# An attention and feed-forward kernel: 15 products for 18 in the feed-forward, key sums on column strips, an inverse root through logarithms

## The chip, the cores and the metric

The kernel runs on one core of one Trainium2 chip. The metric is the time of one execution on the device, in microseconds (us), as the median of several. One execution of each kernel is also recorded by the hardware profiler; its length is called the span and is 1.5 to 3 us under the timed run. The engines are TensorE (PE; PEld are its weight loads), VectorE (DVE), ScalarE (ACT), GpSimd (POOL) and SyncE (SP), which here only issues transfers. A name with a q at its end, such as ACTq, is an engine's own instruction queue issuing transfers.

## The reference, cut

```python
# q, k, v: (8, 12, 448, 64) float32; the weights are float64: 768x1536 twice, 1536x768
rms = np.sqrt(np.mean(x * x, axis=-1, keepdims=True) + 1e-06)
q_n, k_n = q / rms_q * g_q, k / rms_k * g_k          # condensed
attn = np.exp(scale * q_n @ k_n.T - max); attn /= attn.sum(-1) + 1e-9   # condensed
x = (attn @ v) as (B*S, H*D) = 3584 x 768            # condensed
g = x @ w_gate
silu = g * (1.0 / (1.0 + np.exp(-g)))
val = x @ w_val
return (silu * val @ w_out).astype(np.float32)
```

## The kernel before

The program is four blocks of two batches. A block has the gate and value ("up") products, then the output ("down") products. Among the down products of blocks 0, 1 and 2 lies the attention of the next two batches, 12 pairs of heads each: these are the mixed stages. The attention of the first two batches comes ahead of everything, the "early part". Weights are float64 and are converted once, early and beside block 0. A planner in the program lists every operation with a planned cost and time and emits them in an order that it works out; `order.add("DVE", 0.64, when, emit, after=[...])` is one such entry.

The inverse root of the norms, a power on GpSimd:

```python
def inverse():
    rr = take("rr", m, [P, 2 * NC])
    nc.gpsimd.tensor_tensor(out=rr, in0=tiles["ss", m][:, 0], in1=minus_half, op=ALU.pow)
...
rr = add("POOL", 5.2, ready - 14.0, inverse, after=[sums], ...)
```

The sums over keys, four products on 64x64 quarters of TensorE, whose two halves are added and inverted over all 448 queries:

```python
for x in range(2):
    for h in range(2):
        nc.tensor.matmul(
            to[ds(D * h, D), x, 0:S], ones[ds(D * x, D)],
            tiles["sums", m][ds(D * x, D), h], start=True, stop=True,
        )
...
def copy_den():
    nc.scalar.copy(take("inv", m, [P, S]), tiles[den][:, 0, 0:S])

def invert():
    inv = tiles["inv", m]
    nc.vector.tensor_tensor(out=inv, in0=inv, in1=tiles[den][:, 1, 0:S], op=ALU.add)
    nc.vector.reciprocal(inv, inv)
```

The up products, 7 for each 2x2x2 split, with three differences of weights per half-block made on GpSimd:

```python
for to, a, b in ((T1, B12, B11), (T2, B22, T1), (T4, B21, T2), (B12, B22, B12)):
    load = add("POOL", 0.93, ..., lambda ...: nc.gpsimd.tensor_tensor(..., op=ALU.subtract), ...)
...
for c in range(NK):
    nc.tensor.matmul(
        into[:, 0:S], w[:, side, c, :], xs[:, side, c],
        start=(fresh and c == 0), stop=(c == NK - 1), ...
    )
```

## Time and profile before

Three runs: 1548.67 to 1549.82 us, median 1549.4.

| stage | us in the trace |
|---|---|
| early part, to the first dense up product | 138.5 |
| block 0, to the up products of block 1 | 377.9 |
| block 1 | 369.2 |
| block 2 | 370.7 |
| block 3 and the end | 291.6 |
| span | 1547.9 |

A stage begins where the first up product of its block begins. The prediction shows the busy shares, the chain and the stage windows. One view that it doesn't show, the groups of instructions, has the two that the argument needs; the columns are line, engine, operation, out<-in, count | busy us, mean ns of one | idle us of the engine before them and what ended most of it:

```profile
L940 POOL TENSOR_TENSOR rr<-ss,minus_half 128x28 f32<-128x28 f32 x36 | 179.8, 4996 | 122.8 <-DVE ss L934 122.8
L1010 ACT ACTIVATE es<-st 128x896 f32<-128x896 f32 x108 | 95.2, 914 | 137.7 <-PE at L1068 63.2
```

A power over 28 columns costs GpSimd 5.0 us. ScalarE idled 137.7 us before the exponentials, its largest work, and TensorE waited for them only 6.0 us in the whole run: in the mixed stage that the prediction shows, ScalarE is free for more than half of the time.

### The profile page before, as it was taken

Reading aid. Unit: us, or ns where it says so; the run is one execution under the profiler, and the core shown is the slowest. Engines: PE = TensorE matmul, PEld = TensorE weight load, DVE = VectorE, ACT = ScalarE, POOL = GpSimd, SP = SyncE. Lnnn points to the kernel's source line nnn. Section 1 sums busy time; section 2 is a strip of 40 time slices with the busy share of each in tenths; the row PEclk is TensorE's granted clock in tenths of the full one; section 3 lists DMA queues with packets and bytes.
Section 4 is the critical chain, followed back from the end, with each engine's and each line's share of the span. In section 5 each row is a group of like instructions: output and inputs, shape, how many; then the busy total and the mean of one; then the engine's idle time right before and its main releaser. Section 6 shows DMA issues by size and latency. Waiting matters only on the chain.

```text
span 1547.9 us, 17349 instructions
## 1 busy us (share of the span) xinstructions
PE 1507.7 (97%) x6384; PEld 742.4 (48%) x6384; DVE 892.6 (58%) x1053; ACT 449.6 (29%) x761; POOL 726.4 (47%) x440
## 2 busy tenths in 40 slices
PE   6998999999999999999999999999999999999998
PEld 2333544444454555544444555544444455555555
DVE  5999767876676434446777633345577753433221
ACT  6865324334442101233443101013534310000000
POOL 5881356676775222565775332355668433232000
PEclk9999999999999999999999999999999999999999
DMA  6655778734432212333543211233353311111232
GB/s 175 191 169 186 247 232 254 228 111 111 123 79 90 61 41 73 78 78 73 125 94 101 72 43 52 62 80 74 81 120 87 121 61 41 56 47 42 97 112 79
DMA packets 250307, 164.43 MB, mean 106 GB/s; under 512 B 187749, under 2 KB 240229, under 8 KB 249445
## 3 DMA queue, kind: packets, MB, share of 16 engines
q1 hardware_dynamic: 241600, 152.21, 35.1%
q10 hardware_dynamic: 8612, 11.02, 2.1%
q8 instruction: 52, 0.85, 0.2%
q14 instruction: 43, 0.34, 0.1%
HBM read 133.30 MB, written 29.88 MB: 105 GB/s over the span
## 4 chain that ended last, share of the span: by engine, by line
PE 73%; DVE 2%; ACT 1%; DMA 0%; issue 0%; SPq 0%; ACTq 0%; DVEq 0%
PE mm L1318 37%; PE mm L1499 24%; PE st L999 5%; PE at L1068 5%; PE st L1081 2%; ACT es L1010 1%; DVE hs L1467 0%; DMA ws<-out_sides 0%; DVE inv L1114 0%; DVE gt L1467 0%; DVE xs L1155 0%; SPq L886 0%; DVE sums L1021 0%; DVE rows L1576 0%; DVE xs L1123 0%
## 5 line engine op out<-in xcount | busy, mean ns | idle before, releaser
L1318 PE MATMUL mm<-xs,ws 128*128 128x448 f32 x2016 | 764.3, 541 | 8.4 <-DVE xs L1155 4.9
L1318 PEld LDWEIGHTS mm<-xs,ws 128*128 128x128 f32 x2016 | 382.5, 190 | 388.9 <-issue 370.3
L1302 POOL TENSOR_TENSOR ws<-ws 128x384 f32<-128x384 f32 x192 | 207.1, 1089 | 397.5 <-DMA ws<-quarters 350.7
L1499 PE MATMUL mm<-ws,gt 128*128 128x384 f32 x912 | 302.6, 489 | 0.0
L940 POOL TENSOR_TENSOR rr<-ss,minus_half 128x28 f32<-128x28 f32 x36 | 179.8, 4996 | 122.8 <-DVE ss L934 122.8
L1499 PEld LDWEIGHTS mm<-ws,gt 128*128 128x128 f32 x912 | 171.0, 190 | 132.9 <-issue 12.0
L1010 ACT ACTIVATE es<-st 128x896 f32<-128x896 f32 x108 | 95.2, 914 | 137.7 <-PE at L1068 63.2
L1015 POOL TENSOR_TENSOR sums<-es 128x896 f32<-128x896 f32 x36 | 78.2, 2173 | 103.4 <-PE st L1081 50.1
L999 PE MATMUL st<-QT,KT 64*64 64x448 f32 (+1 forms) x1152 | 114.0, 501 | 6.2 <-ACT es L1010 6.0
L1336 DVE TENSOR_TENSOR s<-s,mm 128x448 f32<-128x448 f32 x96 | 59.5, 620 | 99.7 <-PE mm L1318 99.6
L1114 DVE RECIPROCAL inv<-inv 128x448 f32<-128x448 f32 x36 | 106.3, 2953 | 1.2
L1336 DVE TENSOR_TENSOR wide<-s,mm 128x448 f32<-128x448 f32 x72 | 44.7, 621 | 97.7 <-PE mm L1318 97.5
L1336 DVE TENSOR_TENSOR gt<-s,mm 128x448 f32<-128x448 f32 x72 | 44.6, 620 | 93.9 <-PE mm L1318 93.8
L1499 PE MATMUL mm<-ws,hs 128*128 128x384 f32 x288 | 96.4, 490 | 0.0
L1359 ACT COPY s<-mm 128x448 f32<-128x448 f32 x48 | 25.5, 532 | 238.7 <-PE mm L1318 238.7
L1068 PE MATMUL at<-es,v 64*64 64x448 f32 x864 | 88.8, 537 | 0.9 <-DVE xs L1120 0.9
L955 POOL TENSOR_TENSOR t<-qk,rr 128x448 f32<-128x448 f32 x72 | 78.0, 1104 | 1.3
L1015 POOL TENSOR_TENSOR sums<-sums,es 128x896 f32<-128x896 f32 x36 | 75.1, 2086 | 2.8
L1423 ACT ACTIVATE wide<-gt 128x1344 f32<-128x1344 f32 x24 | 31.7, 1323 | 152.8 <-DVE gt L1336 152.7
L1499 PEld LDWEIGHTS mm<-ws,hs 128*128 128x128 f32 x288 | 53.9, 190 | 42.2 <-DVE xs L1120 3.5
L1576 DVE TENSOR_TENSOR rows<-part,mm 128x384 f32<-128x384 f32 x56 | 30.6, 547 | 66.9 <-PE mm L1499 51.2
L1120 DVE TENSOR_TENSOR xs<-xs,at 128x448 f32<-128x448 f32 x36 | 22.3, 619 | 78.0 <-ACT xs L1117 78.0
(93 smaller groups left out, 1352.4 us busy)
## 6 DMA issues: line engine op xcount, KB each, us to landing
ws<-quarters SPq DMA_DIRECT2D x48, 768.0 KB, 4.4
ws<-out_sides SPq DMA_DIRECT2D x28, 1152.0 KB, 6.3
out_sides<-hs SPq DMA_DIRECT2D x6, 1536.0 KB, 6.0
qk<-in_q_dram SPq DMA_DIRECT2D x144, 56.0 KB, 3.0
qk<-in_k_dram SPq DMA_DIRECT2D x144, 56.0 KB, 2.5
out_dram<-rows ACTq DMA_DIRECT2D x42, 192.0 KB, 1.9
stage<-in_moe_w_val_dram SPq DMA_DIRECT2D x10, 768.0 KB, 6.5
v<-in_v_dram SPq DMA_DIRECT2D x72, 96.0 KB, 2.3
```

The costliest lines, as they stand in the source:

```text
L940: nc.gpsimd.tensor_tensor(out=rr, in0=tiles["ss", m][:, 0], in1=minus_half, op=ALU.pow)
L955: nc.gpsimd.tensor_tensor(out=tiles["t", m][:, x], in0=tiles["qk", (m, x)], in1=rr.to_broadcast([P, NC, C]), op=ALU.mult,)
L999: nc.tensor.matmul(st[ds(D * x, D), h, 0:n], tiles["KT", m][rows, ds(P * j + D * of_keys, D)], tiles["QT", m][rows, ds(Q * of_queries, n)] ...
L1010: nc.scalar.activation(e, tiles["st", (m, j)][:, :, 0 : S * width(j) // P], AF.Exp)
L1015: nc.gpsimd.tensor_tensor(out=to, in0=tiles["e", (m, 0)] if j == 1 else to, in1=e, op=ALU.add)
L1068: nc.tensor.matmul(tiles["at", (m, x)][ds(D * h, D), queries], tiles["v", m][rows, j, h], tiles["e", (m, j)][rows, h], start=j == 0, stop= ...
L1114: nc.vector.reciprocal(inv, inv)
L1302: lambda to=to, a=a, b=b: nc.gpsimd.tensor_tensor(out=tiles[key][:, to], in0=tiles[key][:, a], in1=tiles[key][:, b], op=ALU.subtract,),
L1318: nc.tensor.matmul(into[:, 0:S], w[:, side, c, :], xs[:, side, c], start=(fresh and c == 0), stop=(c == NK - 1), skip_group_check=not fina ...
L1336: nc.vector.tensor_tensor(out=to(), in0=one(), in1=two[:, 0:S], op=ALU.add)
L1423: lambda: nc.scalar.activation(take(*wide, [P, 3 * S]), rest, AF.Tanh, scale=0.5),
L1499: nc.tensor.matmul(banks[bank][:, 0:HALF], of(g), w[:, ts(g, HALF)], start=(g == 0), stop=(g == NG - 1),)
```

## The change

It has four intents. The feed-forward is split 2x3x3 with 15 products in place of 18, where before it was 2x2x2 with 7 for 8. All attention, the early part too, runs on 64x64 quarters, and the sums over keys on strips of 128 rows by 32 columns; each gives its sum on 32 partitions, so only 224 columns need inverting, and ScalarE copies the inverse to the partitions that need it. The inverse root moves from GpSimd to ScalarE, as exp(-ln(x)/2), with a refinement on VectorE. In block 0, the rounding of the weights goes through PSUM, which is meant to keep VectorE from locking GpSimd out there. The diff has 1804 lines; its core, shortened:

```diff
-            nc.gpsimd.tensor_tensor(
-                out=rr, in0=tiles["ss", m][:, 0], in1=minus_half, op=ALU.pow
-            )
+        def estimate():
+            ss = of()
+            rr = take("rr", m, list(ss.shape))
+            nc.scalar.activation(rr, ss, AF.Ln, scale=GAIN**-2)
+            nc.scalar.activation(rr, rr, AF.Exp, scale=-0.5)
+        def improve(): ...                # three small VectorE operations
+        first = order.add("ACT", 0.5, when, estimate, ..., mode="logarithms")
 ... key sums of the pairs in the mixed stages
-                        to[ds(D * h, D), x, 0:S], ones[ds(D * x, D)],
-                        tiles["sums", m][ds(D * x, D), h], start=True, stop=True,
+                            to[ds(D * h + C * x, C)], ... many[:, 0:C],
+                            ... term[:, h, ts(x, Q)], start=..., stop=...,
+        def invert():
+            nc.vector.reciprocal(take("rd", m, [P, Q]), tiles[den])
+        def spread():
+            inv = take("inv", m, [P, S])
+            for h in range(2):
+                for x in range(2):
+                    for to in range(2):
+                        nc.scalar.copy(
+                            inv[ds(D * h + C * to, C), ts(x, Q)], tiles["rd", m][ds(D * h + C * x, C)]
+                        )
 ... up products: 15 steps x gate and value x 2 chunks, weight sides made once and stored
+                for c in range(NC2):
+                    nc.tensor.matmul(
+                        ps(), w[:, step % 5, which, c], xs[:, SLOT[x], c],
+                        start=fresh and c == 0, stop=c == NC2 - 1, skip_group_check=True,
+                    )
 ... rounding of the weights
+            if by_bank: ... to = tiles[bank] ...      # a PSUM bank
```

## The prediction

> **What bounds the kernel now.** I read the page's busy shares first, then the chain that ended last in order of time, then the busy time of each engine stage by stage, then the groups by form.
>
> ```profile
> PE 1507.7 (97%) x6384; PEld 742.4 (48%) x6384; DVE 892.6 (58%) x1053; ACT 449.6 (29%) x761; POOL 726.4 (47%) x440
> PE   6998999999999999999999999999999999999998
> ...
> PE 73%; DVE 2%; ACT 1%; DMA 0%; issue 0%; SPq 0%; ACTq 0%; DVEq 0%
> ```
>
> TensorE is busy 97% of 1547.9 us, and the chain that ended last runs over it. Its busy time is modelled, so I look at the pace too. In the chain in order of time:
>
> ```profile
> 516.54 157.99 PE mm L1318 x420
> ...
> 736.11 7.94 PE mm L1499 x24
> ...
> 1256.46 189.56 PE mm L1318 x504
> 1446.02 96.77 PE mm L1499 x300
> ```
>
> L1318 is the gate/value ("up") product, L1499 the output ("down") product. 157.99/420 = 0.376 us for each 448-column instruction, 96.77/300 = 0.323 us for each 384-column one: 0.84 ns a column, without gaps. So the kernel runs at TensorE's rate, and what counts is how many columns TensorE streams. The program is four blocks of two batches: up, then down with the attention of the next two batches mixed in. Up of blocks 1, 2, 3 starts at 516.5, 885.7 and 1254.9, a period of 369.2 us; before it come 12 pairs of heads of early attention and block 0; at the end, up 189.56 + down 96.77 + 5.1 us of last eviction and store.
>
> The other engines in an up stage and in a mixed stage (columns: stretch, length, then busy us of each engine):
>
> ```profile
> 516.50:690.00 173.50, 173.50 (x475) 87.46 (x475) 71.74 (x104) 26.30 (x50) 69.72 (x56) 1.00 0.26 66
> 712.00:885.00 173.00, 171.47 (x1115) 83.91 (x1108) 126.10 (x142) 64.99 (x121) 105.62 (x50) 1.00 0.38 94
> ```
>
> In the mixed stage VectorE is at 126.1/173 = 73%, ScalarE 38%, GpSimd 61%; in up 41%, 15%, 40%. None bounds. The early attention is different: pairs come every 10.6 us (the weighted sums of successive pairs start at 102.49, 113.10 and 123.59), TensorE has about 8.7 us of work in each, and from 40 to 60 us VectorE is busy 19.79 of 20 us. There several engines bind together, and up starts densely at 143.0 with two products (12 instructions) done, as if dense from 138.5.
>
> **What the Trainium skill says.** "FP8 and Floating Point Precision", TensorE Precision Notes: true FP32 takes four passes. The trace agrees: each product is two instructions of 0.376 us for 448 columns, 4 cycles a column at 2.4 GHz within 1%. "TensorEngine Tiling (Array Packing)", Available Configurations and Key Properties: 64x64 gives four tiles, 128x32 four column tiles, and a change of mode drains the array. The trace shows the first: 8 instructions of 448 columns on quarters take two rounds, 0.75 us; it has no 128x32. A cluster from 736.04+7.94 to 750.32 takes 6.34 us against 5.26+0.75 = 6.01 of streaming, so its changes cost about 0.33 us. "ScalarE: Activation LUTs", Table sets: exp and ln share a set, so the new Ln and Exp cost no reload between them; a load is 1283 ns, which the trace's one load shows too. "SBUF — State Buffer", Who interferes with whom: VectorE with two SBUF inputs and GpSimd exclude each other. The trace agrees: the same 448-element operation averages 877 ns with two SBUF operands (L1123), 619 ns with one in PSUM (L1120). Rounding through PSUM avoids that lock in block 0.
>
> **The change part by part.**
>
> Up: now 12 half-blocks x 7 products x 3 chunks x 2 = 504 instructions a block; then 4 groups x 15 products x gate and value x 2 chunks x 2 = 480. At 0.376 that is 180.5 against 189.6: 9.1 us less, four times, all on the path.
>
> Down: now 25 x 6 x 2 = 300 instructions of 384 columns, 96.8 us dense; then 15 x 2 halves x 4 x 2 = 240 of 448, 90.3 us: 6.5 us less, four times. The saving is partly that 3584 tokens are no longer cut into tiles of 128 with one unpaired.
>
> Attention on quarters, 36 pairs: scores and weighted sums stay 5.26 us. The key sums go from 0.75 us to one round of 224 columns twice, 8 instructions on four strips, 2 x 0.188 = 0.376 us. A cluster becomes about 6.01 - 0.376 + 0.33 + 0.2 for one more change of mode = 6.16, against 6.34: 0.2 us x 12 = 2 us a stage.
>
> Mixed stage: now 25 products at 7.94 per two = 99.2, + 12 x 6.34 = 76.1, = 175.3; measured 369.2 - 189.6 = 179.6, so 4.3 us of stalls and small gaps. Then 90.3 + 12 x 0.2 + 12 x 6.16 + 4.3 = 171. Block period 180.5 + 171 = 351.5, against 369.2: 17.7 us less, for two full blocks 35.4.
>
> Last block: 9.1 + 6.5, less about 1.2 for the added 32x32 transpose and 128-byte stores after the last product: 14.4 us less.
>
> Early 12 pairs: TensorE has 5.26 + 1.5 (four key blocks summed by strips) + 0.75 (spreading the reciprocals by product) + about 0.8 for mode changes = 8.3 us, and the two-way halves and 1.2 us of transposes go. VectorE loses half the reciprocal (2.95 to about 1.5, 224 elements) and the sums (1.15), gains two transposes (1.26), three small operations (0.6), a join (0.62): about 6.0 + 6 conversions x 3.7 us/12 = 7.9 against about 9. ScalarE: 7.0 + 1.2 of conversion. GpSimd loses the pow (3 to 5 us) and gains conversion sums. Three engines near 8.3 give about 9.7 us a pair, not the 10.6 of now; 14 + 12 x 9.7 = 130.5, + 8 us for the last pair's reciprocal, division and first side sum, because all first products now need both batches, where the old order began with the even batch: 139. Nothing won, nothing lost.
>
> Block 0: 18 of the 24 weight conversions fall here, each about 4 us of VectorE, 2.4 ScalarE and 7 GpSimd; with evictions (26 of 0.62 us in each of four groups, 65 us) VectorE has some 150 of 190 us. Four accumulators instead of two give each eviction more slack. I allow 12 us of stalls, where the old block 0 lost about 8. Start of up 1: 139 + 180.5 + 12 + 171 = 502.5 against 516.5: 14 us less.
>
> Sum: 1547.9 - 14 - 35.4 - 14.4 = 1484; the timed run is 1.5 above the span: 1485.6. I put 1487.
>
> Removed work that saves nothing by itself: 179.8 + 45.5 us of pow and 207 us of weight differences on GpSimd, and half of 106 us of reciprocals on VectorE; they lay beside TensorE. More DMA (weight sides 1280 KB for each 15 us, 85 GB/s; 128-byte stores) lies under what the page shows it can do, 254 GB/s.
>
> **The rivals.**
> 1. VectorE becomes the bound of the mixed stage. Worked from 126.1: -12 x (1.43 + 0.62) for reciprocal and its add, + 7 for the refinement, + 10 side sums x 0.62, + 7 for 32 evictions and transposes instead of 24, + 12 for the larger combinations of 1792 elements = about 134 of 171, 78%. That is up from 73% but still under TensorE; as queues are in order, some evictions will come late. If each of the 12 clusters lost 1 us: +36 over three stages, 1523.
> 2. ScalarE's new spreading copies (8 of about 0.33 us a pair), store issues (4 of 0.34 us where one was) and table switches delay the exps, and TensorE waits for score banks. Work: 65 + 31 + 2 + 16 = about 114 of 171, from 38% to 67%. For it: nearly all of the PE waits in mixed stages now are already on exps, 6.0 us in total. Against: ample room. Effect 5 to 15 us.
> 3. Block 0 and the early part become bound by conversion and start-up. The program's own planned times allow 10 us a pair instead of 8 and 20 us more for block 0. If early pairs took 11 us and block 0 stalled 25: +29, 1516.
> 4. Strips do not overlap as quarters do: 1.5 us instead of 0.376 in 36 clusters and 6 instead of 1.5 in 12 early ones: about +95, no gain at all. The skill speaks against it.
> 5. Everything overlaps better, since GpSimd's lock on VectorE nearly goes: stalls of 2 instead of 4.3 and an early pace of 9: 1468.
>
> **Range and chances.** The arithmetic on TensorE (36 + 26 us fewer in products) is nearly certain; stalls are not. 1466 to 1514 holds rivals 2, 5 and most of 3. Two per cent faster is 1518.4: only rivals 1 with 3, or 4, cross it. Faster 0.87, same 0.11, slower 0.02.
>
> **What would show it.** Up in the last block about 180.5 us with 480 instructions, the last down about 90.3 with 240; a period of about 351 between up stages; TensorE still about 97% busy and the chain on it; key sums of 8 instructions in about 0.4 us; VectorE under 80% in mixed stages. It is wrong if the period exceeds 358 with waits on VectorE or ScalarE, if the first dense up product starts well after 145, or if the strips take over 1 us.

## The result

The changed kernel takes 1591.17 us (median of 4, 1588.08 to 1595.54), the kernel before 1549.61 in the same rounds: ratio 1.0271, 95% interval 1.0246 to 1.0297, slower. The prediction, 1487 with a range up to 1514, is wrong.

The page of the changed kernel, busy us, share and count by engine, then two lines of the 40 equal slices in tenths:

```profile
PE 1464.4 (92%) x6672; PEld 686.0 (43%) x6672; DVE 903.3 (57%) x1405; ACT 784.7 (49%) x1452; POOL 404.3 (25%) x440
...
PE   3878889999888989999989989999999989999998
...
PEclk9788999999999999999999999999999999999999
```

TensorE has less work, as predicted, but is busy 92% and no longer 97%. GpSimd has 322 us less. ScalarE has 335 us more, 784.7 against 449.6. The slices that lost are in the early part and in the three mixed stages. The granted clock also dips in the early part.

Where do ScalarE's 335 us come from? Its groups, each of one form:

```profile
L978 ACT COPY spare<-rd 32x224 f32<-32x224 f32 x288 | 108.1, 375 | 53.8 <-DVE rd L963 48.1 <-DMA out_dram<-spare 1.3
L667 ACT ACT_TABLE_LOAD x48 | 61.6, 1283 | 0.9
L666 ACT ACT_TABLE_LOAD x47 | 60.3, 1283 | 3.9 <-DMA work<-in_k_dram 3.1
...
L1351 ACT ACT_TABLE_LOAD x9 | 11.5, 1283 | 6.2 <-DVE st L1135 6.1
```

The spreading copies (L978) were expected. The loads of function tables at L666 (the Ln) and L667 (the Exp after it) were not: 95 of them, 121.9 us, where the kernel before has one load in all. L1351 is the Silu. One pair of heads in the timeline (start us, length us, what):

```profile
428.74 0.92 ACT L843 ACTIVATE es<-st 128x896 f32<-128x896 f32 x1
429.67 1.28 ACT L666 ACT_TABLE_LOAD   x1
430.97 0.23 ACT L666 ACTIVATE rr<-ss 128x28 f32<-128x28 f32 x1
431.21 1.28 ACT L667 ACT_TABLE_LOAD   x1
432.50 0.23 ACT L667 ACTIVATE rr<-rr 128x28 f32<-128x28 f32 x1
432.64 0.53 ACT L843 ACTIVATE more<-st 128x448 f32<-128x448 f32 x1
```

An exponential of scores (L843) runs with a table that has Exp. The Ln loads another, the Exp after it loads again, and the next exponential of scores needs none. So the table in use for Exp didn't have Ln, and the one loaded for Ln didn't have Exp. Between the two exponentials of scores, which feed TensorE, lie 2.98 us (429.66 to 432.64), of which 2.57 are loads.

Who waits? TensorE's waits from 700 to 1260 us, which hold two mixed stages, the second of the changed kernel but for its last 51 us (what waited <- for what: us in total, times, longest us). In the kernel before:

```profile
PE st L999 <- ACT es L1010: 4.1, 12, 1.0
```

In the changed kernel:

```profile
PE st L828 <- ACT es L843: 18.9, 19, 3.9
```

The scores (st) wait for a bank that an exponential must first empty. This is the wait that the prediction's second rival named, 15 us more over this window. The mixed stage of block 1 (stretch, length, busy us of PE, PEld, DVE, ACT and POOL, clock, DMA share, GB/s) shows ScalarE at 121.94 of 173 us, 70%, with TensorE at 94%:

```profile
770.00:943.00 173.00, 162.34 (x1044) 71.82 (x1036) 113.98 (x166) 121.94 (x242) 66.35 (x38) 0.99 0.42 94
```

Two steps of the prediction already hold. The down products of the last block, in the chain in order of time, run at the rate assumed, 0.376 us an instruction:

```profile
1496.28 72.17 PE mm L1456 x192
```

An undisturbed cluster of attention is even shorter than predicted. One in the kernel before, with its key sums (L1081) and the next down product (L1499):

```profile
743.98 1.74 PE L999 MATMUL st<-QT,KT 64*64 64x448 f32 x16
...
749.41 0.98 PE L1081 MATMUL st<-sums,ones 64*64 64x448 f32 x8
750.32 0.91 PE L1499 MATMUL mm<-ws,gt 128*128 128x384 f32 x2
```

And one in the changed kernel, with its key sums on strips (L928):

```profile
783.93 1.74 PE L828 MATMUL st<-work 64*64 64x448 f32 x16
...
789.37 0.59 PE L928 MATMUL st<-sums,many 128*32 128x224 f32 x8
789.88 0.64 PE L1456 MATMUL mm<-hs,ws 128*128 128x448 f32 x1
```

From its first scores to the next down product the cluster takes 6.34 us before (750.32 - 743.98) and 5.95 us after (789.88 - 783.93).

### The profile page after: what moved, and what is told of

It is laid out like the page before. It is cut to its first block, busy times and chain, and to the rows that moved or that the text cites. A ratio compares the mean times of both kernels' runs of the same rounds, so it can differ in the third digit from the quotient of the medians.

```text
span 1593.7 us, 19444 instructions
## 1 busy us (share of the span) xinstructions
PE 1464.4 (92%) x6672; PEld 686.0 (43%) x6672; DVE 903.3 (57%) x1405; ACT 784.7 (49%) x1452; POOL 404.3 (25%) x440
## 5 line engine op out<-in xcount | busy, mean ns | idle before, releaser
L1277 PE MATMUL mm<-xs,ws 128*128 128x448 f32 x960 | 408.8, 548 | 21.8 <-DVE xs L1024 8.9
L1277 PE MATMUL at<-xs,ws 128*128 128x448 f32 x960 | 408.5, 549 | 3.8 <-DVE v L1244 3.2
L1277 PEld LDWEIGHTS mm<-xs,ws 128*128 128x128 f32 x960 | 183.9, 193 | 208.6 <-issue 170.0
L1277 PEld LDWEIGHTS at<-xs,ws 128*128 128x128 f32 x960 | 185.2, 193 | 188.7 <-issue 177.5
L783 POOL TENSOR_TENSOR work<-work,rr 128x448 f32<-128x448 f32 x96 | 101.5, 1076 | 649.9 <-DMA v<-in_v_dram 322.0
L828 PE MATMUL st<-work 64*64 64x448 f32 (+1 forms) x1536 | 165.4, 533 | 67.4 <-ACT es L843 31.6
L1456 PE MATMUL mm<-gt,ws 128*128 128x448 f32 x448 | 176.1, 544 | 0.8 <-DVE spare L1244 0.8
L1456 PE MATMUL mm<-hs,ws 128*128 128x448 f32 x384 | 154.3, 553 | 0.0
L1351 ACT ACTIVATE st<-gt 128x448 f32<-128x448 f32 x96 | 52.4, 547 | 196.2 <-DVE gt L1244 94.7
L843 ACT ACTIVATE es<-st 128x896 f32<-128x896 f32 x129 | 114.3, 913 | 50.8 <-PE at L904 20.8
L978 ACT COPY spare<-rd 32x224 f32<-32x224 f32 x288 | 108.1, 375 | 53.8 <-DVE rd L963 48.1
L1456 PEld LDWEIGHTS mm<-gt,ws 128*128 128x128 f32 x448 | 83.5, 190 | 84.6 <-issue 81.8
L1238 ACT COPY gt<-mm 128x448 f32<-128x448 f32 x80 | 42.6, 533 | 156.2 <-PE mm L1277 152.9
```

The source lines that it names most:

```text
L783: nc.gpsimd.tensor_tensor(out=tiles["t", m][:, x], in0=tiles["qk", (m, x)], in1=rr.to_broadcast([P, NC, C]), op=ALU.mult,)
L828: nc.tensor.matmul(st[ds(D * x, D), h, 0:n], tiles["KT", m][rows, ds(P * j + D * of_keys, D)], tiles["QT", m][rows, ds(Q * of_queries, n)] ...
L843: nc.scalar.activation(e, tiles["st", (m, j)][:, :, 0 : S * width(j) // P], AF.Exp)
L978: nc.scalar.copy(inv[ds(D * h + C * to, C), ts(x, Q)], tiles["rd", m][ds(D * h + C * x, C)])
L1238: nc.scalar.copy(to, ps)
L1277: nc.tensor.matmul(ps(), w[:, step % 5, which, c], xs[:, SLOT[x], c], start=fresh and c == 0, stop=c == NC2 - 1, skip_group_check=True,)
```

## The experiments

The theories, as the expectations call them: T1, the table loads are the loss; T2, ScalarE is overloaded by the new copies and stores, loads or not; T3, the early part is slower by its structure; T4, the planner was told 0.5 us for Ln and Exp and so chose a bad order. The first four runs below were made on one chip, with the kernel before at 1549.3 us beside them; the next four (e5 to e8) had it at 1549.98, e9 to e11 at 1549.57 and e12 at 1550.31, so medians can be set side by side to within about 1 us. In e1, e3, e6 and e8 the planner's list and costs stay as they are, so the order of the work does too; the other runs change entries, costs or times in the list, and with them the order. What an order alone can do, e10_plan shows: about 14 us.

**Run e1_one_set: one set of tables that has both functions.** The set is asked for by name before the first Ln or Exp and again after each Silu. Nothing else changes.

```diff
+    def both_functions():
+        if table[0] != "both":
+            nc.scalar.preload_act_table_set("natural_log_exp_and_others")
+            table[0] = "both"
+            both_functions()                       # before the Ln, and before each Exp of scores
             nc.scalar.activation(rr, ss, AF.Ln, scale=GAIN**-2)
+                table[0] = "silu"                  # after each Silu
```

> The changed kernel with one line more before each Ln and Exp that follows a Silu: the table set that holds both is loaded there, so the 96 loads for Ln and Exp fall to about 9, and nothing else changes. Theory T1 (the loads are the cause: 105 loads x 1.283 us = 135 us of ScalarE, in front of exps that TensorE waits for): about 1500 us, early pairs under 11 us apart instead of 12.7, period of a block 352 to 358 instead of 367, granted clock back to 0.99. T2 (ScalarE is overloaded by the 288 spreading copies, 108 us, and the store issues, the loads only fill gaps): 1570 or more, period 363 or more. T3 (the early attention on quarters and the later first product cost the time, not the loads): the first dense up product still starts after 165 and the time stays above 1560.

Measured: 1529.61 us (1527.89 to 1530.3), ratio to the kernel before 0.9873 (0.9857 to 0.989), that is 61.6 us less than the changed kernel and 19.7 less than the kernel before. The loads fall to 18 (9 of this set, 9 for Silu). ScalarE between two exponentials of scores:

```profile
411.29 0.23 ACT L674 ACTIVATE rr<-ss 128x28 f32<-128x28 f32 x1 [3.75 <-DVE ss L778]
411.55 0.23 ACT L675 ACTIVATE rr<-rr 128x28 f32<-128x28 f32 x1
411.68 0.53 ACT L852 ACTIVATE more<-st 128x448 f32<-128x448 f32 x1
```

TensorE's wait for exponentials from 700 to 1260 us is back to what it was before the change, and so is the mixed stage of block 1 (here 724 to 882 us), with TensorE at 98% of it and ScalarE at 64%:

```profile
PE st L836 <- ACT es L852: 3.7, 11, 0.8
```

```profile
724.00:882.00 158.00, 154.95 (x1038) 69.36 (x1033) 112.12 (x164) 100.52 (x225) 66.41 (x38) 1.00 0.44 99
```

So T1 has most of it, though the 1500 us that it expected were missed by 30. T3 falls as the cause of the loss: the first up product comes at 146.0 and not after 165. What is left against the prediction, 42.6 us, is the subject of the later runs.

**Run e2_pow: the inverse root on GpSimd again.** The changed kernel without Ln and Exp for the root, hence without loads too.

```diff
-            nc.scalar.activation(rr, ss, AF.Ln, scale=GAIN**-2)
-            nc.scalar.activation(rr, rr, AF.Exp, scale=-0.5)
+            nc.gpsimd.tensor_tensor(out=rr, in0=ss, in1=minus_half, op=ALU.pow)
```

> The changed kernel with the inverse root back on GpSimd as one pow of 28 elements (about 5 us each, 48 of them) and no Ln, no Exp for it, no refinement on VectorE: no table loads but those for Silu. T1: about 1500 to 1520, a little worse than the run with one set, as pow queues with the weight sums on GpSimd in the early part. T2: 1565 or more. T3: first dense up product after 165.

Measured: 1578.17 us, ratio 1.0191 (1.0174 to 1.0208). The loads are gone, yet it gains only 13 us. The power costs GpSimd 233.5 us, and GpSimd makes the sums of the converted weights:

```profile
L667 POOL TENSOR_TENSOR rr<-ss,minus_half 128x28 f32<-128x28 f32 x48 | 233.5, 4864 | 361.0 <-DVE ss L759 323.9 <-DVE gg L1550 12.4 <-DMA work<-in_k_dram 12.3
```

```profile
PE mm L1266 <- DMA ws<-up_sides: 16.2, 1, 16.2
```

The first up product waits 16.2 us for its weights, and comes at 175.2. T1 had expected 1500 to 1520 here, and what T2 and T3 expected came true, so by itself this run speaks against T1; it removes the loads but puts other work in their place, and the cleaner test is e1_one_set. In the orders that the planner found, moving the root to ScalarE was worth about 48 us (1578.17 - 1529.61), if the two functions share a set; with two sets it lost 13.

**Run e3_before_loads: the loads put into the kernel before.** Two loads more for each pair, and nothing else.

```diff
+            nc.scalar.preload_act_table_set("natural_log")
+            nc.scalar.preload_act_table_set("exp_and_others")
```

> The kernel before with two table loads a pair of heads added on ScalarE at the place of its squared sums (96 loads, 123 us of ScalarE), nothing else. If loads cost by themselves wherever they are, T1 in its plain form: 1549 + about 60 to 100. If they cost only where ScalarE is nearly full (the early part, where it is 70% busy, 10.6 us a pair): early part about 15 to 25 us longer, mixed stages (38% busy) under 3 us each, 1565 to 1580. T2: under 1560.

Measured: 1590.13 us, ratio 1.0264 (1.0247 to 1.0281): 40.8 us for 96 loads, 123 us of ScalarE. By stage: the first up product 22.5 us later, block 0 no longer (396.9 us from its first up product in both), blocks 1 and 2 longer by 10.1 and 8.2. TensorE's waits for exponentials over the whole run, in the mixed stages (L1004) and in the early part (L748):

```profile
PE st L1004 <- ACT es L1015: 22.9, 29, 2.8
PE st L748 <- ACT es L760: 18.7, 9, 4.7
```

The first was 6.0 us in the kernel before. So a load has a price even on a ScalarE that was busy 29%, in an order that was planned without it, since it comes between exponentials for which TensorE waits. The time lies between the two ranges of T1, and the mixed stages lost more than the 3 us each that had been expected.

**Run e4_true_cost: the planner is told the cost of the loads.**

```diff
-            "ACT", 0.5, when, estimate, after=[sums], ...
+            "ACT", 3.1, when, estimate, after=[sums], ...
```

> The changed kernel, loads kept, but the list that fixes the order of the instructions is told 3.1 us for Ln and Exp instead of 0.5. T4 (the order, planned with loads left out, puts exps behind loads at the wrong times; ScalarE has room for them): 1545 or less. T1 in its plain form (the time of the loads itself is the cost): within 10 us of 1591.

Measured: 1593.39 us, ratio 1.0272 (1.0244 to 1.03): the same as the changed kernel, so T4's 1545 or less falls. The stages tell more than the sum. The first up product comes at 201.5 us, 28.0 later than in the changed kernel, but everything after it takes 29.8 us less: 394.6 us for block 0, 358.3 and 357.8 for blocks 1 and 2, 279.7 for the last (402.7, 367.3, 367.2 and 283.0 in the changed kernel). Blocks 1 and 2 are as short as in e1_one_set (357.1 and 355.0), with 32 and 33 loads in them. The same wait from 700 to 1260 us, and the mixed stage of block 1, with ScalarE at 73% and TensorE at 97%:

```profile
PE st L828 <- ACT es L843: 4.2, 12, 1.3
```

```profile
787.00:954.00 167.00, 161.25 (x1048) 69.41 (x1048) 112.95 (x164) 122.47 (x247) 62.27 (x38) 1.00 0.42 95
```

So in the mixed stages an order that reckons with the loads does hide them, and there T4 is right. What the same order loses is the early part, where the first up product waits for its weights:

```profile
PE mm L1277 <- DMA ws<-up_sides: 17.2, 1, 17.2
```

The true cost for the mixed stages alone was not run. An estimate from the stages of these two runs (173.5 us, then 394.6 + 358.3 + 357.8 + 279.7) gives about 1564 us, still above the kernel before.

**Run e5_quarters: strips and spreading undone in the mixed stages.** Taken from e1_one_set; the 36 pairs get the four key sums, the copy, the addition and the full reciprocal of the kernel before.

```diff
+                        nc.tensor.matmul(
+                            to[ds(D * h, D), x, 0:S], ones[ds(D * x, D)],
+                            tiles["sums", m][ds(D * x, D), h], start=True, stop=True,
+                        )
-                "ACT", 2.7, when + 4.5, spread, ...
+                "ACT", 0.55, when + 3.5, copy_den, ...
+                "DVE", 3.6, when + 4.5, invert_all, ...
```

> e1_one_set with the strips and the spreading undone in the 36 pairs of the mixed stages: the sums over keys are four products on 64x64 quarters again (0.76 us of TensorE for some 0.58), one ScalarE copy of 0.55 us in place of eight of 0.375 us, and VectorE adds and inverts over 448 columns (3.6 us for 1.52). Theory T1 (the loads of the function tables were the loss, and with them gone the strips are worth what the prediction says): TensorE gains 36 x 0.2 to 0.35 us = 7 to 13 us of work on the path, so the time is 1537 to 1543 us, against 1530. Theory T2 (ScalarE's spreading copies hold up the mixed stages even without the loads): each of the three mixed stages gets shorter by 5 us or more, and the time is 1515 us or less. Between 1525 and 1535 neither: the strips are a wash.

Measured: 1543.05 us, ratio 0.9955 (0.9941 to 0.9969), against 1529.61 for e1_one_set: strips and spreading together, with the order that comes of them, are worth 13.4 us, 0.37 us a pair. This agrees with the two clusters shown above (0.39 us), but partly by luck. In the profiled runs, 18.7 us apart, blocks 1 and 2 are 6.0 and 7.4 us longer without strips and block 0 is 1.7 shorter, while 7.0 us lie in the early part and the last block, where no pair was changed; and an order alone can do about 14 us. T2 falls: with the loads gone, undoing the eight copies per pair made no stage shorter by 5 us.

**Run e6_loads_early: separate sets in the early part alone.**

```diff
+    def functions(m):
+        if m >= EARLY:
+            both_functions()
+        elif table[0] != "each":
+            nc.scalar.preload_act_table_set("natural_log")
+            table[0] = "each"
```

> e1_one_set, but in the 12 pairs of the early part Ln and Exp have a set each again (about 24 loads of 1.28 us = 31 us of ScalarE), and the shared set in the 36 pairs of the mixed stages. T1: the first up product starts where it does in the changed kernel, at about 173 us instead of 146, and everything after it is as in e1_one_set, so the time is 1530 + 27 = 1557 us; the other 34 us of the 61.6 that the shared set saved belong to the mixed stages, about 11 us to each. Rival: ScalarE's wait in the early part is made good in block 0, which is short of weights then anyway, and the time stays below 1540 us.

Measured: 1555.37 us, ratio 1.0034 (1.0019 to 1.005), 25.8 us above e1_one_set. The first up product comes at 173.9 us, as in the changed kernel (173.5), and block 0 and the later ones have the lengths of e1_one_set. So the early part loses 27 to 28 us to 24 loads (31 us of ScalarE), nearly one for one, and gives none of it back. The rest of the 61.6 us goes, by subtraction, to the loads of the mixed stages in this order; e4_true_cost shows that another order hides them there.

The early part has no slack for it, as the windows from 20 to 146 us show. In e1_one_set:

```profile
20.00:146.00 126.00, 107.17 (x1189) 47.21 (x1186) 93.92 (x157) 86.50 (x165) 56.74 (x83) 0.97 0.70 170
```

In the changed kernel, in the same time:

```profile
20.00:146.00 126.00, 100.75 (x1016) 41.50 (x1008) 74.56 (x129) 104.64 (x175) 51.17 (x76) 0.88 0.58 129
```

ScalarE is at 83%, VectorE has done a fifth less, and TensorE has got through 1016 instructions in place of 1189. Its granted clock is 0.88 for 0.97, which lengthens the instructions too; whether the gaps between its work bring the clock down, no run tests.

**Run e7_one_group: 20 of the 24 weight conversions left out.** A wrong result (relative error 4.6): from e1_one_set, all products read the weights of the first group, as many bytes per load.

```diff
-            make(index, starts[n] + spans[n] * i, ...)
+            if make is up_weights and index < 4:
+                make(index, starts[n] + spans[n] * i, ...)
```

> Wrong result on purpose: e1_one_set with only the first 4 of the 24 weight conversions; all other products read the weights of the first group, with as many bytes per load. Theory: block 0 (from its first up product to that of block 1, 385 us in e1_one_set against 356 in the later ones) is longer because ScalarE, VectorE and the DMA queues convert weights beside it. Then it becomes 356 to 365 us long here and the time is 1500 to 1510 us. Rival: block 0 is longer for another reason (the clock after the start, waits for side sums, the mixed stage's start), then it stays at 380 us or more, and the time at 1522 us or more.

Measured: 1494.14 us, ratio 0.9634 (0.962 to 0.9649). Block 0 takes 352.5 us for 385.0 in e1_one_set, and the first up product comes at 139.5 for 146.0. So the conversions beyond the first group cost 35.5 us by the medians. In the profiled runs they cost 6.5 ahead of the first up product and 32.5 in block 0, of which the later blocks give some 5 back. Without them the kernel lies 7 us above the prediction.

**Run e9_traffic_only: the conversions without their arithmetic.** A wrong result (relative error 1.0): each conversion keeps its load, one ScalarE operation and its store; VectorE's rounding and GpSimd's sums are gone.

```diff
-        for k in range(2):
+        for k in range(0):                 # no rounding on VectorE
...
-            last = add("POOL", us, when, op, after=[last], port=True)
+            pass                           # no sums on GpSimd
```

> Wrong result on purpose: e1_one_set with all 24 weight conversions reduced to their loads, one of the two ScalarE operations and their stores; VectorE's rounding and GpSimd's sums are gone, the bytes that move are the same. It splits what e7_one_group found (block 0 is 385 us long with the conversions beside it, 353 us with 20 of 24 gone). If the transfers are what delays block 0 (DMA share of 0.9 to 0.97 in its first 150 us), it stays at 375 us or more and the time at 1518 us or more. If the arithmetic on VectorE and ScalarE is, block 0 is 350 to 360 us and the time 1490 to 1502 us.

Measured: 1531.93 us, ratio 0.9891 (0.9875 to 0.9906): no better than e1_one_set. The first up product comes at 147.3 us and block 0 takes 381.5 us (146.0 and 385.0 in e1_one_set). The up products of block 0 in three kernels, first e1_one_set, then e7_one_group, then this one:

```profile
146.00:350.00 204.00, 189.55 (x481) 92.55 (x479) 156.59 (x237) 87.26 (x126) 114.92 (x205) 0.97 0.86 266
```

```profile
140.00:327.00 187.00, 185.58 (x528) 91.88 (x527) 83.97 (x146) 64.70 (x120) 9.70 (x8) 1.00 0.31 91
```

```profile
147.00:363.00 216.00, 194.72 (x532) 94.78 (x531) 88.72 (x150) 86.10 (x142) 12.16 (x10) 0.96 0.84 255
```

VectorE falls from 156.59 to 88.72 us of work and GpSimd from 114.92 to 12.16, and the stage even gets longer, by 12 us; some 9 of these are 48 score products of the attention that stand in this stretch here (5.3 us, and 3.9 us of waits before them). The rest of the block is 15.5 us shorter in return, so the block as a whole is 3.5 us shorter. It gets much shorter only in e7_one_group, where the transfers go too, from a DMA share of 0.86 to 0.31, and with them their issues and ScalarE's part. So what this run leaves of the conversions suffices to make the block long: the transfers, their issues on ScalarE's queue and one ScalarE operation each. The waits move: in e1_one_set TensorE waits 13 us in this stage for VectorE's evictions, here 16.3 us for ScalarE's, 13.4 of them in three waits. ScalarE's queue there is taken up by its own issues of stores:

```profile
208.90 4.03 ACTq L1198 DMA_DIRECT2D up_sides<-work  x3
212.97 1.23 ACT L1121 ACTIVATE gt<-gt 128x1152 f32<-128x1152 f32 x1 [5.38 <-issue]
214.23 1.44 ACTq L1194 DMA_DIRECT2D up_sides<-gt  x2
217.20 1.86 ACTq L1198 DMA_DIRECT2D up_sides<-gt  x3
219.11 0.53 ACT L1243 COPY gt<-mm 128x448 f32<-128x448 f32 x1 [4.91 <-DMA up_sides<-gt]
```

Three issues take 4.03 us, and the eviction at 219.11 stands behind them and five more.

**Run e8_gains_queue: the first load of k issued earlier.** From e1_one_set; four small loads go to GpSimd's queue.

```diff
-        nc.scalar.dma_start(t[0:64, :], col)
-        nc.scalar.dma_start(t[64:128, :], col)
+        nc.gpsimd.dma_start(t[0:64, :], col)
+        nc.gpsimd.dma_start(t[64:128, :], col)
```

> e1_one_set with the four small loads of the gains issued from GpSimd's queue rather than ScalarE's, so that ScalarE issues the first load of k about 2.5 us sooner (at 1.6 instead of 4.1 us). If the early part is one chain from the first load on (T3), the first scores come at 15.5 to 16.5 us for 18.1, the first up product 2 us sooner (144 for 146), and the time is 1527 to 1528 us. If the early part is bounded by the work of VectorE and ScalarE per pair, or the load of k is held by the DMA queues and not by its issue, the time stays at 1529 to 1530 us.

Measured: 1529.73 us, ratio 0.9869 (0.9854 to 0.9884): no change. The first up product came 1.5 us sooner (144.5), and block 0 took 388.7 us for 385.0. The head start was not kept; no run says why.

**Run e10_plan: measured lengths in the plan.** From e1_one_set.

```diff
-    LEAD, PAIR = 14.0, 10.0
+    LEAD, PAIR = 14.0, 10.5
-    UP, DOWN, BOTH = 30 * NG * PRODUCT, 90.7, 170.0
+    UP, DOWN, BOTH = 30 * NG * PRODUCT, 90.7, 158.0
```

> e1_one_set with the planned length of the mixed stage at the measured 158 us in place of 170 and 10.5 us for an early pair in place of 10, which changes the order alone. If the wrong plan costs anything (T4 again, now without the loads), the periods shorten by 2 us or more each and the time is 1525 us or less; else it stays within 3 us of e1_one_set's 1529.6 us.

Measured: 1543.16 us (1537.57 to 1546.56), ratio 0.9964 (0.995 to 0.9978): slower than e1_one_set by 13.6 us, a miss of both expectations. Truer lengths made a worse order (block 0 395.7 us, blocks 1 and 2 355.2 and 355.4 in the profiled run). The plan's numbers are settings to try rather than facts to correct.

**Run e11_spaced: the conversions of block 0 over 25 us more.** From e1_one_set.

```diff
-    starts = [LEAD - 4.0, FIRST - 20.0, FIRST + 60.0, FIRST + 110.0]
-    spans = [16.0, 8.0, 9.0, 10.0]
+    starts = [LEAD - 4.0, FIRST - 20.0, FIRST + 70.0, FIRST + 135.0]
+    spans = [16.0, 9.0, 11.0, 12.0]
```

> e1_one_set with the weight conversions of block 0 spread over 25 us more (every 9, 11 and 12 us in place of 8, 9 and 10). If block 0 is long because the conversions crowd VectorE's evictions in the up products (14 us of waits there), its up products get 4 to 10 us shorter; if the mixed stage after it doesn't start later for it, the time is 1521 to 1527 us. Rival: the weights of the down products then come too late, the mixed stage loses what the up products gain, and the time stays at 1530 us or goes above.

Measured: 1526.38 us (1523.43 to 1530.92), ratio 0.985 (0.9833 to 0.9866): the fastest correct kernel here by its median, 3 us below e1_one_set, though the ranges of the two overlap, so I call it no more than level with e1_one_set. The up products of block 0 took 201.7 us for 203.7, not the 4 to 10 us less that were expected.

**Run e12_store_queue: the stores from GpSimd's queue.** From e11_spaced.

```diff
-        queue = nc.scalar if by_bank else nc.sync
+        queue = nc.gpsimd if by_bank else nc.sync
```

> e11_spaced with the stores of the converted weights in block 0 issued from GpSimd's queue in place of ScalarE's. e9_traffic_only showed block 0 just as long with the arithmetic of the conversions gone, with ScalarE's evictions standing behind its own store issues of up to 4 us. If holding ScalarE's queue is the way by which the transfers delay block 0, its up products shorten by 5 to 10 us (201.7 us in e11_spaced) and the time is 1515 to 1522 us. If it is the bandwidth of the DMA engines themselves, or GpSimd's issues now delay its own sums, the time is 1525 us or more.

Measured: 1533.93 us, ratio 0.9902 (0.9881 to 0.9923), slower than e11_spaced. The up products of block 0 took 206.0 us:

```profile
150.00:356.00 206.00, 187.48 (x483) 91.76 (x482) 151.70 (x228) 83.27 (x118) 178.62 (x295) 0.98 0.82 265
```

GpSimd is now busy 178.62 of 206 us, because each of its issues counts as its work. So this run doesn't say whether ScalarE's queue or the DMA engines' share is the way by which the transfers delay block 0; it moved the load to an engine that had no room. That stays open.

## Why the prediction was wrong

The prediction's terms against the traces, each from one first up product to the next (us; the profiled runs' spans):

| term | before | predicted | changed | e4_true_cost | e1_one_set | e7_one_group |
|---|---|---|---|---|---|---|
| first up product | 138.5 | 139 | 173.5 | 201.5 | 146.0 | 139.5 |
| block 0 | 377.9 | 363.5 | 402.7 | 394.6 | 385.0 | 352.5 |
| block 1 | 369.2 | 351.5 | 367.3 | 358.3 | 357.1 | 357.6 |
| block 2 | 370.7 | 351.5 | 367.2 | 357.8 | 355.0 | 358.4 |
| block 3 and end | 291.6 | 278.5 | 283.0 | 279.7 | 283.0 | 284.7 |
| span | 1547.9 | 1484 | 1593.7 | 1591.9 | 1526.1 | 1492.7 |

For the kernel before, the first row is the start that is dense in products. The predicted rows are the prediction's 139, 139 + 180.5 + 12 + 171 = 502.5, its period, and what remains to its 1484.

**The step that failed** is "exp and ln share a set, so the new Ln and Exp cost no reload between them". A set with both exists, and e1_one_set shows that it works. But the program that ran alternated between tables without being asked, 95 loads of 1283 ns. The prediction took what could be loaded for what would be loaded. Sharing the set takes 67.6 us off the profiled span (61.6 by the medians): 27.5 in the early part, 17.7 in block 0, 10.2 and 12.2 in blocks 1 and 2, nothing in the last, which has no pairs. In blocks 1 and 2 the price was that of an order planned without the loads, as e4_true_cost shows; in the early part no order that was tried hid them.

**The second rival was right in kind and too small in size.** It named ScalarE, its "table switches" and waits for score banks, and gave 5 to 15 us. It knew of the switches with Silu alone. Its ScalarE load for a mixed stage, 114 of 171 us, was less than the 121.94 of 173 measured with the loads, and more than the 100.52 of 158 without them, so in sum it was not too small, though a spreading copy took 0.375 us where about 0.33 was given. The chance of 0.02 for slower had only rival 4 (about 95 us) behind it, and the failed sentence had closed the path that was taken. Of the rivals' sums one is wrong: that only rivals 1 with 3, or 4, cross 1518.4 doesn't fit rival 1's own 1523.

**The third rival came true beside it.** It gave 29 us if the early part and block 0 were bound by conversion and start-up. With the table loads gone, the up products of block 1 start at 531.0 us where 502.5 was predicted, 28.5 us late. The next two paragraphs take the two stages one by one.

**Early part.** Predicted 9.7 us a pair, which gave 139. With the loads, it is 173.5. With the shared set 146.0, and with 20 conversions left out 139.5. The prediction had counted six conversions into this part, and that run keeps four of them, so the estimate is met only without the rest. The 6.5 us between these two are conversions that run in it, and since e9_traffic_only begins its up products at 147.3, VectorE's and GpSimd's arithmetic isn't what costs them.

**Block 0.** "I allow 12 us of stalls" is the second mis-sized term. Against 352.5 us without the conversions, e1_one_set's block 0 is 32.5 us longer. The prediction counted VectorE's work, 150 of 190 us, and found room; e9_traffic_only shows that the block is nearly as long with VectorE's and GpSimd's shares removed, so what remains (transfers, their issues on ScalarE's queue, one ScalarE operation) is enough, and no run separates these. A part is TensorE's clock: in the lines above, its 481 instructions take 189.55 us at a granted 0.97, where 528 took 185.58 at 1.00. The prediction put all of the DMA under "what the page shows it can do, 254 GB/s", comparing 85 GB/s of weight loads; with conversions the up products of block 0 moved 266 GB/s, above that figure.

**Blocks 1 and 2.** Predicted 351.5, e1_one_set 357.1 and 355.0. One named part is a wait at the start of each block for the side sums of its last pair, 8.9 us in three waits of 3.0, which the prediction charged to the early part alone. The rest is a few us of clusters and waits that no run separates.

**What held.** Of the four passes that the prediction names, the traces show only the two instructions of a product; no run counts passes. Fewer products at 0.376 us: the last down stage took 90.4 us against 90.3 predicted and 96.9 before. The last up stage took 185.6 us for 180.5 predicted, 3.0 of the difference being the wait just named. Strips overlap; rival 4 falls, and the cluster gained 0.39 us where 0.2 was predicted (its eight products on strips take 0.51 us to the next instruction, 789.37 to 789.88). VectorE stayed at 66% in the mixed stage (113.98 of 173), so rival 1 falls. The 877 ns that the prediction reads for L1123 is a mean raised by a few long ones (median 688, longest 2185), so most of these operations were close to the length with one operand in PSUM (median 621). Last block: 8.6 us less where 14.4 were predicted.

## What to carry to other kernels

When a change brings a second transcendental function to ScalarE, look for table loads in the very first trace, and ask for the shared set by name where one has both functions; that the set exists isn't that it is loaded. An engine at 29% can still set the pace if its new work lies between two results for which the busiest engine waits, so count such work per wait and not as a share, and see what an order that knows of it makes of each stage: one total can hide a gain in three stages and a loss in the first. In a stage that converts data beside its products, count the bytes and the queue that issues them as well as the engines' time.

## What the Trainium skill lacked or had wrong

- "ScalarE: Activation LUTs", Table sets: it gives ln followed by exp as one load, because one set has both. Here it was two loads for every pair of heads, 95 in all, 121.9 us, until the set was named in the program; then 9 loads of it. The page's rules say to use this set; the page lacks that the program had to ask for it. The same page gives each switch 1283 ns and a drain of some 1380 ns; the 1283 ns agree, and a drain is not to be seen: the load starts 0.01 us after the exponential ends (429.66 to 429.67), and the Ln starts 0.02 us after the load.
- "ScalarE activation tables: per-element evaluation and per-set limits", Table sets in the compiler and the runtime: it says that the back end places loads, block by block, by the greedy longest run. A set with both functions would give the longer run between two Silus, and the trace has 95 loads where 9 were enough. Whether something else placed these loads or the rule is another, no run tells.
